# Weights of a network put together from integer halves instead of floating-point products, in a kernel of a gated linear recurrence and a two-layer network

## The chip, the cores and the metric

The kernel runs on one core of a Trainium2 chip. The metric is the time of one launch on the device in microseconds (us), where lower is better. The five engines of a core each work off their own list of instructions, and semaphores hold an instruction until what it needs is there: TensorE (PE) multiplies matrices, VectorE (DVE) and ScalarE (ACT) work element by element, GpSimd (POOL) here clears tiles and issues transfers, and SyncE (SP) only issues transfers.

## The reference

The first half is a recurrence over 768 time steps, for 4 batches and 8 heads of width 48. The second half is a network over the 3072 tokens that come out of it:

```python
f = 1.0 / (1.0 + np.exp(-f_logit))
for t in range(S):
    state = f[:, :, t, :, None] * state + np.einsum('bhd,bhe->bhde', k[:, :, t], v[:, :, t])
    y[:, :, t] = np.einsum('bhd,bhde->bhe', q[:, :, t], state)
...
h = x @ w_in                                          # x is y as (3072, 384); w_in is (384, 2048)
g = np.maximum(h, 0.0) + alpha * np.minimum(h, 0.0)
return (g @ w_out).astype(np.float32)                 # w_out is (2048, 384)
```

`q`, `k`, `v`, `f_logit` and `alpha` are float32. `w_in` and `w_out` are float64, and they arrive in the kernel as 64-bit words which the kernel has to turn into float32 values.

## The kernel before, in words

**Steps.** Time is cut into 6 chunks of 128, and the batches into 2 pairs, which makes 12 steps. Each step has four stages: `prepare` makes products of the decay gates and scaled copies of `q` and `k` (on DVE and ACT); `carry` multiplies across the blocks of a chunk (`off`) and updates the state (`pd`, and `moved`, which writes the state into the tile `vs` on DVE); `attend` computes the scores inside the blocks (`raw`, `qu`), copies them to `A`, multiplies `A` with `vs` (`py`), copies the result to `y` and moves `y` into `xT`, the layout of the network, with ten small transfers (L600 to L608). `network` then computes `ph` = x @ w_in for eight pairs of 128 columns (f0 to f7, L620), the function in the middle with one instruction on ACT (`neg`, L625) and two on DVE (`gate`, L627), and the product with w_out as seven half products that are combined (L655 to L687; the sums of gates that it needs are `sums`, L692). The network of step 0 alone is computed plainly (`po`, L640).

**Order.** PE, DVE and ACT execute in an order that is written out by hand: strings in L726 to L732, one for each of the steps 0 to 3, and one, `usual`, for all others. A letter takes the next piece of a stage: `P` prepare of this step and `Q` of the next, `O` carry, `S` attend, `n` the network of the step before, `a` and `b` the pieces of w_in and w_out on ACT (`uppers`, L232), `w` and `v` the same on DVE (`rests`, L237), `W` the sums of quarters of w_out. A number repeats the letter. The orders of SP and POOL are not written by hand; they follow from where the calls stand in the program.

**Weights.** Each matrix comes in 8 pieces of 128 x 768 words (767 KB, tile `raw`, four buffers), issued by SP. For each piece ACT makes `pos` and `neg` (L202, L204), DVE subtracts them to `lead` (L210, a bf16 value: sign, exponent and first mantissa bits), cuts it to a `power` of two (L216), multiplies the low word by this power (L223, `rest`), and then adds `lead` and `rest`: on DVE for w_in (L228), and by an accumulating transfer issued on POOL for w_out (L230).

**Start.** POOL clears and fills constant tiles, among them the two `vs` (L154 to L157). The first loads of `f`, `q`, `k` and `vs` are issued on SP (L265, L279). PE runs 40 groups of small matmuls on constants (L746)[...].

**Banks.** `psa` has two buffers of two PSUM banks ("pair"), shared by `raw`, `qu`, `off`, `pd` and `py` in turn; so `qu` of a step can start only when the tile before the last has been read completely, for instance `pd` by `moved`. `psn` has four single banks for the network.

Of the kernel before, what the change touches and what calls it, by code (L numbers as in the profile page):

```python
# [8 lines left out]
F32 = mybir.dt.float32  # L9
I16 = mybir.dt.int16  # L10
U16 = mybir.dt.uint16
BF16 = mybir.dt.bfloat16
I32 = mybir.dt.int32
U32 = mybir.dt.uint32
AF = mybir.ActivationFunctionType
ALU = mybir.AluOpType
# [5 lines left out]
U = 2  # L22
CH = 64
NC2 = C // CH
NB = DB // 4
WP = 768
AT_ONCE = 8
IDLE = 40
RAWS, TOPS, POWERS, LEADS = 4, 3, 1, 4


@with_exitstack
def kernel(
# [30 lines left out]
    nc = tc.nc  # L64
    B, NC, _, HP, _ = qT.shape
    DM = v.shape[-1]
# [6 lines left out]
    W = U * HP * C  # L73
# [15 lines left out]
    const = ctx.enter_context(tc.tile_pool(name="const", bufs=1))  # L89
    work = ctx.enter_context(tc.tile_pool(name="work", bufs=2))  # L90
    staging = ExitStack()
    stage = staging.enter_context(tc.tile_pool(name="stage", bufs=1))
# [3 lines left out]
    def pair(name):  # L96
        return psa.tile([128, 2, 512], F32, tag="pair", name=name)

    def bank(name):
        return psn.tile([128, 512], F32, tag="net", name=name)  # L100
# [8 lines left out]
    nc.scalar.dma_start(out=om, in_=alpha)  # L109


    kr = const.tile([128, W // 4, 4], F32, tag="kr", name="kr")
    nc.gpsimd.memset(kr[:, :, 3:4], 1.0)
    NS = G * (NB + 1) + 1
# [20 lines left out]
    for m in range(1, NB):  # L135
        lo = UO[m] + (4 if m == 1 else 0)
        n = NB - m
# [4 lines left out]
    for half in range(2):  # L142
        for m in range(1, NQ):
            n = NQ - m
# [6 lines left out]

    A = const.tile([128, U, H, C], F32, tag="A", name="A")
    nc.gpsimd.memset(A, 0.0)
    vs = []  # L154
    for bp in range(B // U):
        vs.append(const.tile([128, NC2, U, DM + 16], F32, tag=f"vs{bp}", name=f"vs{bp}"))
        nc.gpsimd.memset(vs[bp], 0.0)  # L157
    ident = const.tile([128, 128], F32, tag="ident", name="ident")
    make_identity(nc, ident)
    nc.gpsimd.tensor_scalar(om, om, -1.0, 1.0, ALU.mult, ALU.add)  # L160
# [7 lines left out]
    def load_weights(dst, src, name):  # L168

        rows_ = NK if dst is w_in_sb else 1  # L180
        pieces_ = dst.shape[1] * dst.shape[2] // WP
        if rows_ == 1:
            dst = dst.rearrange("p a n -> p (a n)").unsqueeze(1)
        width = WP // rows_
        words = src.rearrange("p (a n) -> p a n", a=rows_).bitcast(I16)
        at_once = AT_ONCE if rows_ > 1 else 0
        got = {}

        def of(n):
            return dst[:, :, n * width:(n + 1) * width]  # L190

        def by_row(t):
            return t.rearrange("p (a n) -> p a n", a=rows_)

        def upper(n):
            raw = stage.tile([128, WP, 4], I16, tag="raw", name=f"{name}_raw{n}", bufs=RAWS)
            nc.sync.dma_start(out=raw.rearrange("p (a n) four -> p a (n four)", a=rows_)[:, :, 0:4 * width - 1],
                              in_=words[:, :, 4 * n * width + 1:4 * (n + 1) * width])

            top = raw[:, :, 2]  # L200
            pos = stage.tile([128, WP], I16, tag="pos", name=f"{name}_pos{n}", bufs=TOPS)
            nc.scalar.activation(pos, top, AF.Relu, bias=bias[:, 0:1], scale=8.0)  # L202
            neg = stage.tile([128, WP], I16, tag="wneg", name=f"{name}_neg{n}", bufs=TOPS)
            nc.scalar.activation(neg, top.bitcast(U16), AF.Relu, bias=bias[:, 1:2], scale=8.0)  # L204
            got[n] = raw, pos, neg

        def lead(n):
            raw, pos, neg = got[n]
            t = stage.tile([128, WP], BF16, tag="lead", name=f"{name}_lead{n}", bufs=LEADS)
            nc.vector.tensor_tensor(t, pos.bitcast(BF16), neg.bitcast(BF16), ALU.subtract)  # L210
            got[n] = raw, t

        def power(n):
            raw, t = got[n]
            p = stage.tile([128, WP], BF16, tag="power", name=f"{name}_power{n}", bufs=POWERS)
            nc.vector.tensor_scalar(p.bitcast(I16), t.bitcast(I16), -128, None, ALU.bitwise_and)  # L216
            got[n] = raw, t, p

        def rest(n):
            raw, t, p = got.pop(n)  # L220
            got[n] = t
            low = raw.bitcast(U32)[:, :, 0]
            nc.vector.scalar_tensor_tensor(of(n), by_row(low), 2.0 ** -36, by_row(p), ALU.mult, ALU.mult)  # L223

        def both(n):
            t = by_row(got.pop(n))
            if n < at_once:
                nc.vector.tensor_tensor(of(n), of(n), t, ALU.add)  # L228
            else:
                nc.gpsimd.dma_start(out=of(n), in_=t, accum_op=ALU.add)  # L230

        def uppers():  # L232
            for n in range(pieces_):
                upper(n)
                yield

        def rests():  # L237
            for n in range(pieces_ + 1):
                if n < pieces_:
                    lead(n)  # L240
                if n:
                    rest(n - 1)
                if n < pieces_:
                    power(n)
                if n:
                    both(n - 1)
                yield

        return uppers(), rests()

    def rows(par):
# [257 lines left out]
    def attend(bp, c, x):  # L509
# [6 lines left out]
        for u in range(U):  # L516
            raw = pair(f"raw{u}_{i}")
# [9 lines left out]
            for d in range(4):  # L527
                n = 4 - d
# [11 lines left out]
            if c:  # L540
                for m in range(1, NB):
                    lo = UO[m] + (4 if m == 1 else 0)
                    n = DB - 4 * m
# [4 lines left out]
            else:  # L548
                qv = qu.rearrange("p r (h x) -> p (r h) x", h=HP)
                adh = ad[:, u].rearrange("p r h (a t) -> p (r h) a t", a=2)  # L550
                for m in range(1, NQ):
                    n = 4 * (NQ - m)
                    lo = 4 if m == 1 else VO[m]
                    hi = lo + (DB - 4 if m == 1 else 2 * n)
                    to, of, by = ad[:, u].rearrange("p r h t -> p (r h) t")[:, :, 4:DB], qv[:, :, lo:hi], mhalf[:, lo:hi]
                    by = by.bitcast(I32).unsqueeze(1).broadcast_to((128, H, hi - lo))
                    if m > 1:
                        to = adh[:, :, :, 4 * m:16]
                        of, by = (t.rearrange("p h (a t) -> p h a t", a=2) for t in (of, by))
# [11 lines left out]
        for u in range(U):  # L571
            for hp in range(HP):
                for cc in range(NC2):
                    for par in range(2):
                        hd = 2 * hp + par
# [12 lines left out]
        if not (bp or c):  # L588

            for kt in range(NK):  # L590
                b = bank(f"xt{kt}_{i}")
                pairs = [hp for hp in range(HP) if 2 * D * hp < 128 * (kt + 1) and 2 * D * (hp + 1) > 128 * kt]
                for hp in pairs:
                    o = 2 * D - 2 * D * hp + 128 * kt
                    nc.tensor.matmul(b[:, 0:T], lhsT=dense[:, o:o + 128], rhs=y[:, :, hp],
                                     start=(hp == pairs[0]), stop=(hp == pairs[-1]))
                nc.scalar.copy(xT[:, kt], b[:, 0:T])
            yield
            return
        for hd in range(H):  # L600
            d = hd * D
            while d < (hd + 1) * D:
                n = min((hd + 1) * D, (d // 128 + 1) * 128) - d
                p0 = 64 * (hd % 2) + d - hd * D
                (nc.sync if hd % 2 else nc.scalar).dma_start(
                    out=xT[d % 128:d % 128 + n, d // 128].rearrange("p (u t) -> p u t", u=U),
                    in_=y[p0:p0 + n, :, hd // 2])
                d += n  # L608
# [94 lines left out]
    def halves_of_w_out():  # L703
# [12 lines left out]
        for to, x_, y_, op in ((t3, b22, b12, ALU.subtract), (t2, t3, b11, ALU.add), (t4, t2, b21, ALU.subtract),  # L716
                               (b12, b12, b11, ALU.subtract)):
            for h in range(2):
# [5 lines left out]

    steps = [(bp, c) for c in range(NC) for bp in range(B // U)]
    first = (  # L726
        "P2 a P w P a P2 a w a w O a w S2 Q O S Q w S a Q S w S",
        "P n b P a w a n O b w2 v2 S P b n3 v S b2 S2 v2 n Q b n2 Q O b v b n v2 n v S W Q2 S Q W n Q W n W",
        "n2 S n W n3 S n2 Q O S n O Q2 S n S Q S n Q2 n2",
        "S n2 S Q n2 O n O S2 n3 Q2 S n2 S Q n Q n2 Q",  # L730
    )
    usual = "S n2 S n O n O n Q n3 Q n Q S3 n Q S n Q n Q n"  # L732
    pieces = {key: part for keys, parts in (("aw", load_weights(w_in_sb, w_in, "w_in")),
                                            ("bv", load_weights(w_out_sb, w_out, "w_out")))
              for key, part in zip(keys, parts)}

    pieces["W"] = halves_of_w_out()

    def begin(n):
        if n >= len(steps):  # L740
            return [None] * 4
        x = {}
        return [stage(*steps[n], x) for stage in (prepare, carry, attend, network)]

    with tc.manual_schedule(engines={mybir.EngineType.PE, mybir.EngineType.DVE, mybir.EngineType.Activation}):
        for _ in range(IDLE):  # L746
            nc.tensor.matmul(idle[0:32, 0:8], lhsT=ones[:, 0:32], rhs=ones[:, 0:8], start=True, stop=True)
# [65 lines left out]
```

## Time and profile before

| | |
|---|---|
| time, median of 3 runs | 631.77 us (630.31 to 632.38) |
| profiled execution: its own time | 629.98 us |
| profiled execution: span | 628.2 us, granted clock 0.978 |
| busy: PE / PE weight loads / DVE / ACT / POOL | 590.1 / 525.2 / 512.1 / 248.7 / 58.5 us |
| first ph matmuls, `raw` of step 1 starts | 50.5 us, 61.3 us |
| `po` of step 0 | 86.4 to 109.8 us |
| `raw` of steps 3, 5, 6, 7 starts | 160.2, 254.8, 302.1, 349.5 us |
| last matmul ends | 624.9 us |

The profile is of one execution. Its span is counted from the first to the last instruction. "PE off L447 <- DVE q L371: 11.8, 1, 11.8" in the list of waits says that PE stood 11.8 us in total, once, before the instruction of line 447 that works on `off`, and that the wait ended with DVE's instruction of line 371. A releaser called "issue" means that the profile shows nothing that was waited for. In the slices of the span each digit is the busy share of a fortieth of it (15.7 us) in tenths. In a timeline the columns are start, duration, engine, line, operation, tiles, and in brackets the idle time before it. SPq and ACTq are the times in which SP and ACT issue transfers.

### The profile page before, as it was taken

Reading aid. Unit: us, or ns where it says so; the run is one execution under the profiler, and the core shown is the slowest. Engines: PE = TensorE matmul, PEld = TensorE weight load, DVE = VectorE, ACT = ScalarE, POOL = GpSimd, SP = SyncE. Lnnn points to the kernel's source line nnn. Section 1 sums busy time; section 2 is a strip of 40 time slices with the busy share of each in tenths; the row PEclk is TensorE's granted clock in tenths of the full one; section 3 lists DMA queues with packets and bytes.
Section 4 is the critical chain, followed back from the end, with each engine's and each line's share of the span. In section 5 each row is a group of like instructions: output and inputs, shape, how many; then the busy total and the mean of one; then the engine's idle time right before and its main releaser. Section 6 shows DMA issues by size and latency. Waiting matters only on the chain.

```text
span 628.2 us, 19015 instructions
## 1 busy us (share of the span) xinstructions
PE 590.1 (94%) x8188; PEld 525.2 (84%) x8188; DVE 512.1 (82%) x1035; ACT 248.7 (40%) x466; POOL 58.5 (9%) x107
## 2 busy tenths in 40 slices
PE   2458899998999999999999999999999999999997
PEld 2447776788889889889889889889889889889997
DVE  5999799999888889888888888889888889762261
ACT  5766592343451243244244244244244244223110
POOL 9020123001001001001001001001001000000000
PEclk9958799999999999999999999999999999999999
DMA  7944698223313313313313323323323211201000
GB/s 250 314 142 147 178 291 185 29 64 108 70 59 85 84 38 86 69 52 86 71 50 85 67 56 78 55 74 85 54 68 86 47 41 27 53 3 26 26 0 26
DMA packets 70323, 53.57 MB, mean 85 GB/s; under 512 B 47296, under 2 KB 62144, under 8 KB 70240
## 3 DMA queue, kind: packets, MB, share of 16 engines
q1 hardware_dynamic: 57536, 25.37, 16.1%
q0 software_dynamic: 7312, 24.78, 14.1%
q10 hardware_dynamic: 5392, 2.21, 1.8%
q8 instruction: 65, 1.06, 0.8%
q14 instruction: 18, 0.15, 0.1%
HBM read 36.21 MB, written 4.72 MB: 65 GB/s over the span
## 4 chain that ended last, share of the span: by engine, by line
PE 64%; DVE 17%; ACT 10%; issue 4%; DMA 3%; ACTq 1%; DVEq 0%; SPq 0%
PE ph L620 26%; PE pc L659 9%; PE pa L659 6%; PE pe L659 5%; PE pd L659 5%; PE qu L538 3%; ACT A L566 3%; PE raw L523 3%; DVE S L701 3%; DVE gate L627 3%; DVE qd L290 3%; PE py L577 2%; ACT us L317 2%; DMA xT<-y 2%; PE po L640 2%
## 5 line engine op out<-in xcount | busy, mean ns | idle before, releaser
L620 PE MATMUL ph<-xT,w_in_sb 128*128 128x256 f32 x1152 | 262.2, 385 | 0.9 <-DMA xT<-y 0.9
L620 PEld LDWEIGHTS ph<-xT,w_in_sb 128*128 128x128 f32 x1152 | 217.0, 191 | 34.2 <-issue 3.1
L625 ACT ACTIVATE neg<-ph 128x512 f32<-128x512 f32 x96 | 57.1, 596 | 195.5 <-PE ph L620 148.2
L627 DVE SCALAR_TENSOR_TENSOR gate<-neg,om,ph 128x256 f32<-128x256 f32 x192 | 82.1, 476 | 49.1 <-ACT neg L625 48.9
L659 PE MATMUL pc<-t,S 128*128 128x192 f32 x352 | 61.7, 329 | 0.0
L659 PE MATMUL pa<-w_out_sb,gate 128*128 128x192 f32 x352 | 61.1, 327 | 0.0
L659 PEld LDWEIGHTS pa<-w_out_sb,gate 128*128 128x128 f32 x352 | 57.9, 190 | 0.6
L659 PEld LDWEIGHTS pc<-t,S 128*128 128x128 f32 x352 | 57.3, 190 | 0.6
L422 ACT COPY A<-q 48x512 f32<-48x512 f32 x44 | 27.2, 617 | 52.4 <-DVE q L371 52.0
L544 DVE COPY_PREDICATED ad<-mquad,qu 128x224 f32<-128x224 int32 (+6 forms) x140 | 41.9, 299 | 6.2
L529 DVE COPY_PREDICATED ad<-mraw,raw 128x256 f32<-128x256 int32 (+1 forms) x96 | 42.3, 441 | 3.1 <-PE raw L523 0.6
L566 ACT COPY A<-ad 32x256 f32<-32x256 f32 x96 | 38.5, 401 | 1.8 <-DVE ad L560 0.4
L333 DVE TENSOR_TENSOR us<-us,fs 128x768 f32<-128x768 f32 (+5 forms) x60 | 36.7, 611 | 0.0
L677 ACT COPY o<-pa 128x192 f32<-128x192 f32 x11 | 3.5, 319 | 81.2 <-PE pa L659 74.9
L577 PEld LDWEIGHTS py<-A,vs 128*64 128x64 f32 x768 | 25.8, 145 | 9.6 <-ACT A L566 6.8
L577 PE MATMUL py<-A,vs 128*64 128x64 f32 x768 | 29.2, 233 | 4.9 <-ACT A L566 4.2
L659 PE MATMUL pe<-w_out_sb,S 128*128 128x192 f32 x176 | 30.5, 327 | 2.4 <-ACT o L677 2.4
L659 PEld LDWEIGHTS pe<-w_out_sb,S 128*128 128x128 f32 x176 | 28.8, 190 | 2.7 <-ACT o L677 2.7
L538 PE MATMUL qu<-us,k 48*32 48x112 f32 (+1 forms) x1536 | 27.4, 260 | 3.7 <-issue 3.5
L701 DVE TENSOR_TENSOR S<-gate 128x512 f32<-128x512 f32 x44 | 30.3, 688 | 0.8
L659 PE MATMUL pd<-w_out_sb,S 128*128 128x192 f32 x176 | 30.4, 326 | 0.0
L659 PE MATMUL pb<-t,gate 128*128 128x192 f32 x176 | 30.4, 326 | 0.0
(110 smaller groups left out, 729.7 us busy)
## 6 DMA issues: line engine op xcount, KB each, us to landing
w_out_raw<-in_w_out SPq DMA_DIRECT2D x8, 767.8 KB, 6.6
w_in_raw<-in_w_in SPq DMA_DIRECT2D x8, 767.2 KB, 5.6
f<-in_fT POOLq DMA_DIRECT2D x11, 512.0 KB, 4.8
q<-in_qT POOLq DMA_DIRECT2D x11, 512.0 KB, 4.1
k<-in_kT POOLq DMA_DIRECT2D x11, 512.0 KB, 4.6
out<-o SPq DMA_DIRECT2D x24, 192.0 KB, 2.7
vs<-in_v POOLq DMA_DIRECT2D x22, 192.0 KB, 4.9
w_out_sb<-w_out_lead POOLq DMA_DIRECT2D x8, 384.0 KB, 6.9
```

Of the source, the lines that this page charges most:

```text
L333: nc.vector.tensor_tensor(us[:, :, UO[m]:UO[m] + 4 * n].rearrange("p g (i r) -> p g i r", r=4), us[:, :, skip:skip + 4 * n].rearrange("p g ...
L422: nc.scalar.copy(A[halves(cc)[1], :, par * HP:(par + 1) * HP, CH * cc:CH * (cc + 1)], q3[rows(par)].rearrange("p (u h c) s t -> p u h c (s ...
L529: nc.vector.copy_predicated(adu[:, :, :, d:4], mraw[:, d, :, d:4].bitcast(I32).unsqueeze(1).broadcast_to((128, H, NB, n)), rv[:, :, QO[d]: ...
L538: nc.tensor.matmul(qu[DB * j:DB * (j + 1), par, hp * QS + 4:hp * QS + QL], lhsT=k4[r_, g * DB:(g + 1) * DB], rhs=us[r_, g, 4:QL], start=Tr ...
L544: nc.vector.copy_predicated(ad[:, u, :, :, 4 * m:DB], mquad[:, lo:lo + n].bitcast(I32).unsqueeze(1).unsqueeze(1).broadcast_to((128, 2, HP, ...
L566: nc.scalar.copy(A[s_, u, :, s_], ad[s_, u].rearrange("p r h t -> p (r h) t"))
L577: nc.tensor.matmul(py[64 * par:64 * par + 64, u, o:o + CH], lhsT=vs[bp][:, cc, u, hd * D:hd * D + 64], rhs=A[:, u, par * HP + hp, CH * cc: ...
L620: nc.tensor.matmul(ph[:, j * T:(j + 1) * T], lhsT=w_in_sb[:, kt, m * 128:(m + 1) * 128], rhs=xT[:, kt], start=(kt == 0 and j == 0), stop=( ...
L625: nc.scalar.activation(neg, phv, AF.Relu, scale=-1.0)
L627: nc.vector.scalar_tensor_tensor(gate[:, m % NH, m // NH], neg[:, j], om[:, m:m + 1], phv[:, j], ALU.mult, ALU.add)
L659: nc.tensor.matmul(to[:, 0:DH], lhsT=of(f), rhs=by(f), start=(f == 0 and not more), stop=(f == NH - 1), skip_group_check=True)
L701: nc.vector.tensor_tensor(to, x_, y_, op)
```

## The change

It has six parts. (1) ACT gets a third instruction for each piece: it scales the low word by 2^-13 and rounds it to a 32-bit integer in the final weight tile. `power` and `rest` on DVE are gone, and `both` adds `lead`, read as a 16-bit integer, to the upper half of each 32-bit weight. (2) This holds for w_out too, so its eight accumulating transfers on POOL are gone. (3) The two `vs` tiles are cleared on DVE at the very beginning instead of on POOL. (4) 56 instead of 40 groups of small matmuls run at the start. (5) The ten transfers to `xT` go round SP, ACT, POOL, SP, ACT instead of SP and ACT in turn. (6) All five order strings are new.

```diff
-AT_ONCE = 8
-IDLE = 40
-RAWS, TOPS, POWERS, LEADS = 4, 3, 1, 4
+IDLE = 56
+RAWS, TOPS, LEADS = 4, 3, 4
...
+    vs = []
+    for bp in range(B // U):
+        vs.append(const.tile([128, NC2, U, DM + 16], F32, tag=f"vs{bp}", name=f"vs{bp}"))
+        nc.vector.memset(vs[bp], 0.0)
+
     kr = const.tile([128, W // 4, 4], F32, tag="kr", name="kr")
...
-    vs = []
-    for bp in range(B // U):
-        vs.append(const.tile([128, NC2, U, DM + 16], F32, tag=f"vs{bp}", name=f"vs{bp}"))
-        nc.gpsimd.memset(vs[bp], 0.0)
...
+            nc.scalar.activation(as_int(n, I32), by_row(raw.bitcast(U32)[:, :, 0]), AF.Copy, scale=2.0 ** -13)
             got[n] = raw, pos, neg
 
+        def as_int(n, dtype):
+            t = of(n).bitcast(dtype)
+            return t if dtype is I32 else t.rearrange("p a (n two) -> p a n two", two=2)[:, :, :, 1]
...
-        def power(n):
-            raw, t = got[n]
-            p = stage.tile([128, WP], BF16, tag="power", name=f"{name}_power{n}", bufs=POWERS)
-            nc.vector.tensor_scalar(p.bitcast(I16), t.bitcast(I16), -128, None, ALU.bitwise_and)
-            got[n] = raw, t, p
-
-        def rest(n):
-            raw, t, p = got.pop(n)
             got[n] = t
-            low = raw.bitcast(U32)[:, :, 0]
-            nc.vector.scalar_tensor_tensor(of(n), by_row(low), 2.0 ** -36, by_row(p), ALU.mult, ALU.mult)
 
         def both(n):
-            t = by_row(got.pop(n))
-            if n < at_once:
-                nc.vector.tensor_tensor(of(n), of(n), t, ALU.add)
-            else:
-                nc.gpsimd.dma_start(out=of(n), in_=t, accum_op=ALU.add)
+            t = by_row(got.pop(n).bitcast(I16))
+            nc.vector.tensor_tensor(as_int(n, I16), as_int(n, I16), t, ALU.add)
...
+        queues = iter([nc.sync, nc.scalar, nc.gpsimd, nc.sync, nc.scalar] * 2)
...
-                (nc.sync if hd % 2 else nc.scalar).dma_start(
+                next(queues).dma_start(
...
     first = (
-        "P2 a P w P a P2 a w a w O a w S2 Q O S Q w S a Q S w S",
-        "P n b P a w a n O b w2 v2 S P b n3 v S b2 S2 v2 n Q b n2 Q O b v b n v2 n v S W Q2 S Q W n Q W n W",
-        "n2 S n W n3 S n2 Q O S n O Q2 S n S Q S n Q2 n2",
-        "S n2 S Q n2 O n O S2 n3 Q2 S n2 S Q n Q n2 Q",
+        "P5 a w P a2 O w S w a w a2 S Q S O S w Q2 S Q2 S w",
+        "a2 w b w O w n2 b2 v S P v2 n2 S b v Q n b n O S2 v n b v n Q2 b v Q b n S v2 W Q W S n2 W n W",
+        "n S P n2 S n W n O Q n3 O S Q n S Q n S Q2 S Q n3",
+        "S n3 P S Q S n O n O n4 Q S Q S Q n S Q n3",
     )
-    usual = "S n2 S n O n O n Q n3 Q n Q S3 n Q S n Q n Q n"
+    usual = "S n2 O P n S Q n2 Q n3 O n S2 n Q S Q2 S n3"
```

## The prediction

> **What bounds the kernel now.** I read the share of busy time first, then the slices of the span.
>
> ```profile
> PE 590.1 (94%) x8188; PEld 525.2 (84%) x8188; DVE 512.1 (82%) x1035; ACT 248.7 (40%) x466; POOL 58.5 (9%) x107
> ...
> PE   2458899998999999999999999999999999999997
> ...
> DVE  5999799999888889888888888889888889762261
> PEclk9958799999999999999999999999999999999999
> ```
>
> TensorE (PE) is the bound: 628.2 - 590.1 = 38 us idle, and the windows place 31 us of it before 130 us, 2.4 at 155 to 157.5, about 1.2 from 160 to 580, and 3.2 behind the last matmul. A usual step repeats every 47.33 us (`raw` starts at 254.78 and 302.11) with some 47.24 of it matmuls. So there are two places to look at: the first 130 us, where something can be won, and the usual step, where at most 0.1 us can be won but anything late costs seven times (steps 4 to 10). VectorE (DVE) reads 9 in nearly every early slice, so it looks like the bound there. The waits say what PE stood for, and where ACT did:
>
> ```profile
> PE off L447 <- DVE q L371: 11.8, 1, 11.8
> ...
> PE off L457 <- issue: 5.5, 2, 3.8
> ...
> PE qu L538 <- issue: 3.5, 2, 2.0
> ...
> ACT w_in_pos L202 <- DMA w_in_raw<-in_w_in: 3.2, 1, 3.2
> ...
> PE pe L659 <- ACT o L677: 2.4, 1, 2.4
> ```
>
> The first is step 0's own preparation on DVE, which the change leaves. The fourth has its origin on SP's queue, the fifth on ACT's (timelines of the two):
>
> ```profile
> 2.26 0.69 SPq L197 DMA_DIRECT2D w_in_raw<-in_w_in  x1
> 8.61 1.31 SPq L279 DMA_DIRECT2D vs<-in_v  x2
> 9.96 12.91 SPq L197 DMA_DIRECT2D w_in_raw<-in_w_in  x4
> ```
>
> ```profile
> 150.90 5.90 ACTq L605 DMA_DIRECT2D xT<-y  x5
> 157.14 0.32 ACT L677 COPY o<-pa 128x192 f32<-128x192 f32 x1 [6.27 <-DMA xT<-y]
> ```
>
> The `vs` loads wait on SP until POOL has cleared `vs` (8.61); the second weight piece stands behind them and lands at 16.05. At 150.9 ACT needs 5.9 us to issue five transfers and only then copies `pa`, for which `pe` waits. Five issues take 0.6 us each; single issues in step 4 show a gap from 245.00 to 248.25 before the fifth, just after the first landings at 248.0: the 9th and 10th of the ten transfers wait until the first ones land.
>
> **What the Trainium skill says.** "VectorE: DVE Perf Modes", What auto-detection actually checks: a two-source operation runs two elements a cycle only when every tensor is 16-bit with step 1 or -1. The trace agrees: `lead` (bf16, contiguous) takes 551 ns, the f32 add of 768 elements 952. The new int16 add has step 2, so it should be a 952. "DMA: Bandwidth & Descriptors", Issuing engines are not separate DMA queues: a third queue saves issue time on the sequencer and no transfer time; the trace shows landings after 4.9 us (median) against 0.6 us for an issue. "TensorE: Matmul & The Clock Gate", Part 1: an idle window halves the clock. PEclk shows it: 0.51 at 40 to 50 us and 0.50 at 60 to 70.
>
> **The parts.**
> *Weights, DVE.* Each of 16 pieces loses `power` (0.36) and `rest` (0.95). `both` stays at 0.95 for w_in's eight and is new on DVE for w_out's eight. Starts follow each other about 0.09 closer than durations. w_in: 8 x 1.31 = 10.5 us less; w_out: 8 x (0.36 + 0.95 - 0.95) = 2.9 less. DVE gains 13 us. Unknown is the int16 add: 0.5 if it ran packed, 1.9 at double; I take 0.95.
>
> *Weights, ACT.* A third instruction per piece, a Copy of 768 without a bias pointer. Copies of 512 take 0.590 and of 1024 1.042 (rows `ksn` and `qd`), so between them 0.82; "ScalarE: Activation LUTs", What ACT_TABLE_LOAD costs, prices 186 + 0.833 x 768 = 826 ns, an estimate. Bounds 0.72 and 1.05 (pos measures 0.99). 16 x 0.82 = 13 us more on ACT: the work is not removed, it changes engine. It stands in front of `A`, `us` and `y` copies there, so in the first 60 us it is not free.
>
> *Accumulating transfers.* Eight of 384 KB leave POOL's queue (6.9 us to landing). They compete with the xT transfer of 110 us, which took 7.75 us to land and cost PE 0.9.
>
> *Memsets of vs.* From POOL (1.43 us each) to DVE's head. "VectorE: DVE Perf Modes", Zero memsets, says one cycle an element: 1600 elements, about 1.7 us each, an estimate no row here shows. DVE first works at 4.2 us, waiting for `lvl` and `f`: 3.4 fits. Without that cover it would cost its 3.4. SP then goes f, q, k, vs, raws without a stop: raw 1 can land near 10 instead of 16, and ACT's 3.2 us wait falls away.
>
> *IDLE 56.* 16 more groups at the start, while PE waits for `off` until 21 anyway. The 3.84 us "issue" stall at 21 to 24.8 falls on the first long run of matmuls while DMA is 0.9 busy[...]. I let it vanish, but `off` itself is not the end of that chain, so it counts zero. Bounds 0 and -2.
>
> *Step 0 walked through.* ACT is now the chain from `A<-q` at 20.6: pieces 1, 2 (2 x 2.55) to 25.9; off and ksn copies to 28.8; pieces 3 to 5 (7.5) to 36.3; f, kr, qd to 39; `A<-ad`, vs, `A<-ad` to 43.2; `us` to 45.3; y to 46.4; xT to 51.6; pieces 6, 7 and w_out's first (7.6) to 59.2; `off` evicted 61.1, and `raw` of step 1 at 61.2 against 61.34. Nothing is won up to here: ACT took back what DVE gave. What is won comes after it, while PE runs the 36 `ph` matmuls and `po` of step 0: the 2.04 us `qu` L538 <- issue stall at 63 (the same shift of fetches as above), the half clock at 60 to 70 us in which 36 `ph` matmuls took 10.24 us instead of 8.0, and the 0.9 for xT; together 5.2, of which I count 4.5 because the half clock follows idle time that may move and not go. `po` ends at about 105.5 instead of 109.8. Gain 4.5, bounds 2 (half clock and xT wait stay or move) and 6 (a `raw` 1 us earlier).
>
> *n = 2.* L677 now follows four issues (2.8 us; no slot to wait for), so the 2.4 us stall goes. DVE, with w_out's adds and W behind it, may hold qu1 up by 1.0. Gain 1.4, bounds 0 and 2.4.
>
> *xT on three queues.* SP 4, ACT 4, POOL 2. ACT's issue falls from 5.9 to 2.8 us, which in a usual step hides nothing (L677 at 297.02, `pe` at 299.42). POOL's two stand behind the `vs` loads, which wait for `py`; landing at about 47 + 2 against need at 49.0 within the period. Zero, bounds 0 and 0.5 a step.
>
> *The usual order.* This is the row I distrust. Lines of DVE in the step at 254.78:
>
> ```profile
> 280.87 2.48 DVE L627 SCALAR_TENSOR_TENSOR gate<-neg,om,ph 128x256 f32<-128x256 f32 x6
> ...
> 291.89 0.36 DVE L672 TENSOR_TENSOR Csum<-pc,Csum 128x192 f32<-128x192 f32 x1 [1.45 <-PE pc L659]
> ...
> 296.85 1.12 DVE L501 TENSOR_TENSOR vs<-vs,pd 48x384 f32<-48x384 f32 x2
> ...
> 303.91 0.43 DVE L529 COPY_PREDICATED ad<-mraw,raw 128x256 f32<-128x256 int32 x1
> ```
>
> Gates of f7 end 28.6 us into the step, and pa's last weights (its matmuls start 26.5 in, 2.6 long) need them at 28.5 to 28.7: no slack already. In the new order the `A<-q` copies (2.5 us, ACT) stand before neg f2 and Q1 (3.64) before gates f3; I find f7's gates at 29.0, 0.3 to 0.5 late. `moved(1)` now comes after Q3, Q4 and Q5: from L672 at 34.45, 3.13 + 3.66 + 4.45 + 2.1 + the 0.27 of L676 = 13.6, to 48.0; `qu` u0 of the next step takes the pair that `moved(1)` frees and would start at 47.92. So 0.1 to 0.2 late. DVE has 4.7 us of slack in a step (42.4 of 47.3 us), so lateness isn't carried on. Together 0.4 a step, x 7 = 2.8 us lost; bounds 0 and 8. The drained steps 11 and 12 and the tail stay.
>
> **Sum.** -4.5 - 1.4 + 2.8 = -3.1 us. The profiled execution took 629.98 (span 628.2 and 1.8 around it), so 626.9; the median of the runs lies 1.8 above the profiled one, 631.77 - 3.1 = 628.7. I say 628.5.
>
> **Rivals.**
> *Slower side: DVE's late moved(1) and gates bound every usual step.* Place: `qu` u0 of steps 5 to 11 and pa's last weights. It decides when DVE's chain ends over 1.0 us late a step: 7 x 1.1 = 7.7 lost against 4.5 won in the prologue if the n = 2 gain is eaten by qu1: 631.77 + 3.2, about 635. For it: both slacks are already nil or below. Against it: DVE has 4.7 us idle a step, which the new order may place better than I see.
>
> *DVE bounds the first 70 us.* Then 13 us less work on it is worth 8 to 10, giving about 622. For it: the 9s. Against: ACT's walk above, which is full from 20.9 on.
>
> *ACT takes back everything, or the int16 add runs at 1.9.* Each 0.1 us more on the Copy costs 0.9 on the nine pieces before step 1; at 1.05 it costs 2, the usual loss 2.8, so the time stays within a microsecond of 631.8.
>
> **Chances.** Forecast (623.5 to 629.8): 0.46. More, as in the second rival: 0.12. Unchanged: 0.18. Slower: 0.24. A measurement of this kernel tells about 0.3% (1.9 us) from nothing. Faster 0.58, same 0.18, slower 0.24. The range goes from 621.5 (most of the larger gain) to 636 (most of the slower rival), and leaves 0.2; the likeliest case alone has 623.5 to 629.8.
>
> **What would show it.** Right: no ACT wait for w_in_raw; ACT without gaps from 21 to 60; `raw` of step 1 within 1 us of 61.3; po's end 4 to 5 us earlier; no pe wait at 155; steps of 47.7 in place of 47.33, with PE waiting for DVE before pa or qu. Wrong: steps of 47.3 or below (then 625.5 or so), or above 48.2 (then slower); int16 adds far from 0.95 or Copies far from 0.82; a `raw` of step 1 that moves by several us either way.

## The result, and the profile after

The changed kernel takes 627.39 us (median of 5 runs, 626.62 to 628.11) against 630.58 us for the kernel before (median of 5 runs that now include the three shown above, 629.81 to 632.38). The ratio is 0.9943, with a 95% interval of 0.9923 to 0.9962: 0.57% faster. Its profiled execution took 627.25 us with a span of 625.4 us, 2.8 us shorter than the one of before.

The page of the changed kernel, shares of busy time and slices of the span:

```profile
PE 590.1 (94%) x8220; PEld 525.8 (84%) x8220; DVE 502.5 (80%) x1013; ACT 265.3 (42%) x482; POOL 60.5 (10%) x119
...
PE   3458999999999999999999999999999999999997
...
DVE  7599889999799599699699699699799789663261
ACT  5797893361442542442443343353253253222110
PEclk9996999999999999999999999999999999999999
```

DVE lost 9.6 us of busy time and ACT gained 16.6; PE's busy time is what it was. DVE reads 5 in the second slice (16 to 31 us), where it read 9, and ACT reads 9 in the third (31 to 47 us), where the page of before has a 6. The list of waits, the lines in which PE or the weights figure:

```profile
PE off L432 <- DVE q L356: 9.3, 1, 9.3
...
PE raw L508 <- ACT A L450: 5.2, 1, 5.2
...
PE pd L472 <- issue: 2.4, 1, 2.4
...
PE qu L523 <- DVE vs L486: 2.0, 5, 0.4
...
PE qu L523 <- DVE ad L529: 1.3, 1, 1.3
```

There is no wait of ACT for `w_in_raw` any more, and none of `pe` for L663 (the old L677). Three new ones stand there: PE for ACT in step 0 (5.2 us), PE for DVE in step 2 (1.3 us, at 118.2), and `qu` for `moved(1)` in five usual steps, 0.4 us each. (The diff of the change further up has a slip in the string of step 2: the kernel that ran ends it with `Q n S Q n Q S2 Q n3`.)

The two places that the prediction showed, in the timelines of SP and ACT of the changed kernel:

```profile
2.56 1.42 SPq L264 DMA_DIRECT2D vs<-in_v  x2
4.02 20.28 SPq L196 DMA_DIRECT2D w_in_raw<-in_w_in  x6
```

```profile
149.58 2.82 ACTq L591 DMA_DIRECT2D xT<-y  x4
152.50 0.32 ACT L663 COPY o<-pa 128x192 f32<-128x192 f32 x1 [2.95 <-DMA xT<-y]
```

And the end of a usual step on DVE, with the `qu` that stands behind it on PE:

```profile
285.82 0.36 DVE L658 TENSOR_TENSOR Csum<-pc,Csum 128x192 f32<-128x192 f32 x1 [0.72 <-PE pc L645]
...
298.40 1.12 DVE L486 TENSOR_TENSOR vs<-vs,pd 48x384 f32<-48x384 f32 x2
...
300.75 0.35 DVE L672 TENSOR_TENSOR o<-pe,o 128x192 f32<-128x192 f32 x1
```

```profile
298.25 0.92 PE L508 MATMUL raw<-qd,k 48*32 48x80 f32 x64
299.58 1.11 PE L523 MATMUL qu<-us,k 48*32 48x112 f32 x64 [0.41 <-DVE vs L486]
```

How the start of `raw` moved from the kernel before to the changed one shows where the time went (us, the two profiles):

| | before | after | difference |
|---|---|---|---|
| `raw` of step 1 | 61.34 | 64.80 | +3.5 (`ph` of f0 and f1 are done by then in both) |
| start of the first `po` | 86.39 | 84.57 | -1.8 |
| `ph` behind the last `po` | 109.61, and 0.89 of wait for xT in it | 107.42, no wait | -2.2, with the wait -3.1 |
| `raw` of step 3 | 160.31 | 156.36 | -3.95 |
| `raw` of step 5 | 254.78 | 250.65 | -4.13 |
| `raw` of step 10 | 491.55 | 489.02 | -2.53 |
| start of the last product `pe` | 622.08 | 619.35 | -2.73 |

Between steps 5 and 10 a step takes 47.67 us instead of 47.35. From the start of `raw` of step 1 to the first `po`, with the same matmuls in both kernels, PE takes 19.8 us instead of 25.1. What makes `raw` of step 1 late is seen on PE (timeline of the changed kernel):

```profile
55.95 1.97 PE L459 MATMUL pk<-ident,ks 128*128 128x128 f32 x8
57.71 7.17 PE L606 MATMUL ph<-xT,w_in_sb 128*128 128x256 f32 x24
64.80 0.92 PE L508 MATMUL raw<-qd,k 48*32 48x80 f32 x64
```

The granted clock is 0.67 in these 10 us (50 to 60). At full clock 24 such matmuls take 5.45 us, for instance from 66.24 on.

### The profile page after: what moved, and what is told of

It is laid out like the page before. It is cut to its first block, busy times and chain, and to the rows that moved or that the text cites. A ratio compares the mean times of both kernels' runs of the same rounds, so it can differ in the third digit from the quotient of the medians.

```text
span 625.4 us, 19119 instructions
## 1 busy us (share of the span) xinstructions
PE 590.1 (94%) x8220; PEld 525.8 (84%) x8220; DVE 502.5 (80%) x1013; ACT 265.3 (42%) x482; POOL 60.5 (10%) x119
## 4 chain that ended last, share of the span: by engine, by line
PE 70%; DVE 19%; ACT 8%; issue 1%; DMA 1%; ACTq 0%; DVEq 0%
PE ph L606 37%; PE pa L645 8%; PE pc L645 7%; PE pb L645 4%; PE qu L523 3%; PE pe L645 2%; PE pd L645 2%; DVE us L318 2%; PE raw L508 2%; PE py L562 1%; PE pd L472 1%; DVE q L356 1%; DVE us L309 1%; DVE k L335 1%; DVE vs L486 1%
## 5 line engine op out<-in xcount | busy, mean ns | idle before, releaser
L645 PE MATMUL pa<-w_out_sb,gate 128*128 128x192 f32 x352 | 63.4, 333 | 0.0
L645 PE MATMUL pc<-t,S 128*128 128x192 f32 x352 | 60.9, 326 | 0.0
L514 DVE COPY_PREDICATED ad<-mraw,raw 128x256 f32<-128x256 int32 (+1 forms) x96 | 42.4, 442 | 8.3 <-PE raw L508 5.8
L551 ACT COPY A<-ad 32x256 f32<-32x256 f32 x96 | 38.6, 402 | 1.4
L571 ACT COPY y<-py 128x512 f32<-128x512 f32 x24 | 12.9, 592 | 58.1 <-PE py L562 58.1
L302 ACT COPY us<-qd 128x256 f32<-128x256 f32 x48 | 29.8, 675 | 7.6 <-DVE qd L275 7.5
L508 PEld LDWEIGHTS raw<-qd,k 48*32 48x32 f32 x1536 | 18.3, 109 | 14.3 <-issue 8.7
L508 PE MATMUL raw<-qd,k 48*32 48x80 f32 x1536 | 23.3, 243 | 7.1 <-ACT A L450 5.2
```

What stands on the lines that cost most here:

```text
L302: nc.scalar.copy(q4[:, :, :, r], qdv[r][:, :, :, 0])
L508: nc.tensor.matmul(raw[DB * j:DB * (j + 1), par, hp * C:hp * C + QW], lhsT=k[r_, g * DB:(g + 1) * DB], rhs=qd[r_, g], start=True, stop=True)
L514: nc.vector.copy_predicated(adu[:, :, :, d:4], mraw[:, d, :, d:4].bitcast(I32).unsqueeze(1).broadcast_to((128, H, NB, n)), rv[:, :, QO[d]: ...
L551: nc.scalar.copy(A[s_, u, :, s_], ad[s_, u].rearrange("p r h t -> p (r h) t"))
L645: nc.tensor.matmul(to[:, 0:DH], lhsT=of(f), rhs=by(f), start=(f == 0 and not more), stop=(f == NH - 1), skip_group_check=True)
```

## The experiments

Each was timed in five rounds beside the kernel before, whose median in these rounds was 630.8 to 631.0; the number beside each result is its ratio to the kernel before with the 95% interval. The changed kernel stands at 0.9943.

**The usual order undone.** Only the last two lines of the order change.

```diff
-        "S n3 P S Q S n O n O n4 Q S Q S Q n S Q n3",
+        "S n3 P S Q S n O n O n4 Q S Q S Q n S Q n3 Q",
...
-    usual = "S n2 O P n S Q n2 Q n3 O n S2 n Q S Q2 S n3"
+    usual = "S n2 S n O n O n Q n3 Q n Q S3 n Q S n Q n Q n"
```

> The changed kernel with the usual order of the kernel before (and one more Q at the end of step 3's string, which that order needs). Theory (the new usual order loses about 0.4 us a step because qu waits for moved(1)): the waits of qu for L486 are gone, steps fall from 47.67 to 47.35 us, and the time from 627.4 to about 625.2 us. Rival (the new weights and queues also need the new usual order, for instance because xT is late): a new wait in every usual step, and 627.4 or more.

Measured: 625.41 us, 0.9924 (0.9906 to 0.9942). `raw` starts at 296.91, 344.33 and 391.70, steps of 47.4, and no `qu` waits for L486. The theory held: the new usual order costs 1 to 2 us (2.0 between the medians, 1.2 between the two ratios to the kernel before), and the new weights and queues do not need it.

**moved(1) put earlier.**

```diff
-    usual = "S n2 O P n S Q n2 Q n3 O n S2 n Q S Q2 S n3"
+    usual = "S n2 O P n S Q n2 Q n3 O n S2 n Q S2 Q2 n3"
```

> The changed kernel with one piece moved in the usual order: the last piece of attend (y, moved(1), the xT transfers) before the last two pieces of the coming step's prepare instead of after them, so that on VectorE moved(1) runs some 5 to 8 us earlier. Theory (the 0.41 us wait of qu in five or six steps is moved(1) alone): steps of 47.3, the time about 2 us below the changed kernel, 625.3. Rival (VectorE is simply late as a whole and another instruction is waited for next, such as the q3 product that the score copies need): below 0.7 us gained.

Measured: 630.22 us, 1.0005 (0.9992 to 1.0018), 2.8 us slower than the changed kernel, so the theory fell in this form. The wait of `qu` is gone, but the next one is longer (waits of PE, and the timelines of DVE and PE, of this run):

```profile
PE ph L606 <- DVE Csum L667: 6.9, 6, 1.2
```

```profile
291.16 0.95 DVE L482 TENSOR_TENSOR vs<-vs,f 48x768 f32<-48x768 f32 x1 [0.95 <-PE py L562]
...
301.72 0.35 DVE L667 TENSOR_TENSOR Csum<-pc,Csum 128x192 f32<-128x192 f32 x1
```

```profile
302.13 5.45 PE L606 MATMUL ph<-xT,w_in_sb 128*128 128x256 f32 x24 [1.22 <-DVE Csum L667]
```

`moved(1)` now stands at DVE's head before `py` is through, so DVE idles 0.95 us, and everything behind it is that much later. The last in line are the combinations of the half products, and L667 frees the bank that `ph` of f0 takes. In the changed kernel that instruction ended at 300.2, 0.4 us ahead of `ph`. The rival was right: the step's end has two releases to serve, a pair for `qu` and a bank for `ph`, and moving one alone makes the other late.

**Both releases ahead of the fifth piece.** The end of the usual order is mixed so that `moved(1)` and the combinations both come before the 4.4 us of the fifth piece of `prepare`.

```diff
-    usual = "S n2 O P n S Q n2 Q n3 O n S2 n Q S Q2 S n3"
+    usual = "S n2 O P n S Q n2 Q n3 O n S2 n Q S Q S n2 Q n"
```

> The changed kernel with the end of the usual order mixed on VectorE: the fourth piece of prepare, then y and moved(1), then the combinations of the half products, then the fifth piece, then the last combination. The run that put moved(1) first made the combinations 1.2 us late for the bank of ph f0; here both come before the fifth piece (4.4 us). Theory (the loss of a usual step is which of VectorE's releases come last, not its amount of work): no wait of PE for L486 or L667, steps of 47.3, about 625.2 us as with the old usual order. Rival (VectorE's list is too long for the end of the step in any order that begins with Q pieces this late): some wait of 0.3 us or more a step remains, 627 or more.

Measured: 624.91 us, 0.9909 (0.9894 to 0.9924). Steps of 47.3 (`raw` at 296.95, 344.33, 391.53, 438.88), no wait of PE for L486 or L667 in a usual step. So it is which release comes last that costs, and not the amount of work on DVE, which is the same in this and the two kernels above.

**xT on two queues again.**

```diff
-        queues = iter([nc.sync, nc.scalar, nc.gpsimd, nc.sync, nc.scalar] * 2)
+        queues = iter([nc.scalar, nc.sync] * 5)
```

> The changed kernel with the xT transfers on SyncE and ScalarE in turn, as before. The prediction priced three queues at zero in a usual step. Theory A (that price holds, and only step 2 gains): 2.4 us lost once, 629.8. Theory B (the new order has py later, so that y is copied 5 us before pe instead of 10, and ScalarE's five issues of 5.9 us delay L663, for which pe waits): about 2 us lost in each of eight steps, 16 us, 643 us, with PE waiting at pe for L663.

Measured: 629.85 us, 0.9988 (0.9972 to 1.0004). The size is that of theory A and the mechanism that of theory B:

```profile
PE pe L645 <- ACT o L663: 5.5, 7, 1.5
```

`pe` waits in seven steps, 0.3 to 1.5 us each, and not in step 2 alone (there 0.51). ACT's five issues took 4.2 to 5.3 us in these seven steps, where step 2 of the kernel before had 5.9. The transfers land sooner in the new order (2.7 us in the median against 4.7), which fits the prediction's reading that the last issues wait for the first landings. The waits of `qu` for L486, 2.0 us in the changed kernel, are gone in this run, so the two do not add: on balance the third queue is worth 2.5 us in the new order, a little in each step.

**Three queues alone in the kernel before.**

```diff
+        queues = iter([nc.sync, nc.scalar, nc.gpsimd, nc.sync, nc.scalar] * 2)
...
-                (nc.sync if hd % 2 else nc.scalar).dma_start(
+                next(queues).dma_start(
```

> The kernel before with the xT transfers on three queues alone. Theory (ScalarE's issue falls from 5.9 to 2.8 us, and only step 2 has pe waiting behind it): 2.4 us faster than before, 628.2 to 628.6, no wait of pe for L677 left. Rival (the wait passes on to the next instruction, for instance to VectorE's combinations or to xT behind GpSimd's vs loads): below 1 us gained.

Measured: 631.4 us, 1.0007 (0.9994 to 1.002). The rival held. ACT's issues did fall to 2.8 us and `pe` no longer waits, but in the same step PE then stands for DVE (timeline of PE of this run):

```profile
162.75 1.08 PE L538 MATMUL qu<-us,k 48*32 48x112 f32 x64 [0.94 <-DVE us L333]
165.08 5.45 PE L621 MATMUL ph<-xT,w_in_sb 128*128 128x256 f32 x24 [1.26 <-DVE Csum L682]
```

0.94 + 1.26 = 2.2 of the 2.4 us are back: DVE must have been about 2 us late in the kernel before too, where the stall covered it. From the start of `pe` of step 2 to the next `pe` this run takes 49.42 us, where the kernel before takes 46.95.

**Fewer groups at the start.** `IDLE = 40` in place of 56.

> The changed kernel with 40 instead of 56 groups of small matmuls at the start. Theory (these only move the places where PE's stalls named issue fall): the three stalls named issue of the changed kernel (0.6 at 32.9, 2.4 at 36.9, 1.3 at 55.2) move to other instructions, and the time changes by less than 1 us, 626.4 to 628.4. Rival (the extra groups took away the 3.8 us stall that the kernel before had at 21 us): the stall is back, raw of step 0 starts later, and the time rises by 2 us or more.

Measured: 626.8 us, 0.9947 (0.9926 to 0.9969), no difference. The rival's stall did come back: PE's waits of this run show `off` L442 <- issue with 4.8 us, 3.7 of them at once, and the 5.2 us wait of `raw` for ACT that the changed kernel has is only 1.25 us here: the stall lies in the same time. `raw` of step 0 starts at 27.85 us, as in the changed kernel (27.77), so PE stood for ACT's list either way.

**The integer weights alone, in the kernel before.** Its function `load_weights` is replaced by the new one (parts 1 and 2 of the change, the diff above), all else stays.

> The kernel before with the integer weights alone (parts 1 and 2 of the change; order strings, memsets, 40 groups and two queues as before). Theory (ScalarE takes back in the first 60 us what VectorE gives, and the order around it is the old one): raw of step 1 within 1.5 us of 61.3, the time within 2 us of the kernel before. Rival (VectorE was the bound of the first 70 us): 4 to 8 us faster.

Measured: 634.86 us, 1.0063 (1.0046 to 1.0081): 0.6% slower than the kernel before. Neither theory allowed for this. `raw` of step 1 starts at 67.28 instead of 61.34: ACT's additional Copies stand before `off`'s evictions, and PE waits for these (`raw` <- ACT A L449, 3.64 us at step 0 and 1.86 at step 1), while DVE, relieved of 10.9 us of busy time, stands for `lead`'s inputs (6.4 us). ACT also waits 6.0 us for `w_in_raw`, in two waits, but that is no effect of the new weights: the profile of the three-queue run above, which has the old ones, shows the same 6.0 us and `raw` of step 1 at 64.60. Beside that profile the integer weights are 2.7 us later, about as much as the three Copies (0.9 us each) that ACT makes from 59 us on, ahead of the evictions of `off` of step 1. So about 3 of the 4 us are placed, in ACT's Copies, and the remaining 1 us stays open. (That both profiles are 3.3 us or more behind that of the kernel before at this place is not the weights' doing: the three-queue run shows it without them.)

**The floating-point weights in the changed kernel.** Its `load_weights` is replaced by the old one.

> The changed kernel with the weights put together as before (power, rest, and w_out's accumulating transfers on GpSimd). Theory (the weights are worth little by themselves, the gain is order and queues): 1 to 3 us slower than the changed kernel, 628.5 to 630.5. Rival (the new order needs the 13 us that VectorE was given): VectorE is full past 70 us, moved and the gates are late in the first three steps, 633 or more.

Measured: 637.86 us, 1.011 (1.0094 to 1.0126), 10.5 us slower than the changed kernel, and the rival held, though in part elsewhere than it said. Half of the loss is there at `raw` of step 1, which starts at 69.57 us and not at 64.80 (timelines of ACT and SP and waits of PE in this run):

```profile
38.50 0.98 ACT L203 ACTIVATE w_in_pos<-w_in_raw,bias 128x768 int16<-128x768 int16 x1 [7.37 <-DVE ad L561]
```

```profile
24.38 10.74 SPq L198 DMA_DIRECT2D w_in_raw<-in_w_in  x3
```

```profile
PE pd L488 <- issue: 5.3, 1, 5.3
...
PE py L578 <- ACT A L567: 4.8, 2, 4.5
...
PE po L642 <- DMA w_out_sb<-w_out_lead: 1.7, 1, 1.7
```

The instruction named as the releaser of ACT's 7.37 us is not the cause: it belongs to another chain and ends at 38.6. The sixth piece needs the `raw` buffer of the second, which in this form is read last by DVE's `rest`; that ended at 31.9, SP issued the load at 31.98 (the second of the three issues shown), and it landed 6.4 us later, at 38.39. With the new weights ACT is the last reader and frees the buffer itself. So the order, in which ACT takes six pieces before `y`, stands on that, and `f`, `A` and `y` were queued behind the 7.4 us. (At 66.14 ACT has stood another 7.0 us, for a `pos` buffer that DVE's `lead` frees.) (DVE's own time for a piece, 2.6 us against 1.4, did not fill it: it was idle 2.7 us at 38.6.) From `raw` of step 1 to `raw` of step 2 another 4.5 us are lost: the granted clock is 0.83 from 60 to 80 us, so that 24 `ph` matmuls take 6.90 us and not 5.45, and `po` waits 1.7 us for one of w_out's accumulating transfers. `raw` of step 3 starts at 166.03 instead of 156.36. So neither the weights nor the rest of the change is a gain by itself: +4.0 and +7.0 us, and together -3.2. What the new form is worth for w_in and for w_out singly was not run.

**Two pieces put into ACT's gap.** The trace of the changed kernel shows ACT idle from 13.8 to 19.84 us, waiting for DVE's `q` product, with the words of pieces 1 and 2 landed at 14.3 and 16.8:

```profile
19.84 1.25 ACT L407 COPY A<-q 48x512 f32<-48x512 f32 x2 [6.06 <-DVE q L356]
```

```diff
-        "P5 a w P a2 O w S w a w a2 S Q S O S w Q2 S Q2 S w",
+        "P5 a3 w P O w S w a w a2 S Q S O S w Q2 S Q2 S w",
```

> The changed kernel with w_in's pieces 1 and 2 moved on ScalarE ahead of the score copies of step 0 (A from q), into the 6.1 us in which ScalarE waits for these; the pieces' words have landed at 14.3 and 16.8 us. Nothing else moves. Theory (ScalarE's list is the chain from 20 us to raw of step 1): everything on ScalarE after 21 us is about 5 us earlier, so y at about 41 instead of 45.6 and raw of step 1 at about 60 instead of 64.8; the time 3 to 5 us lower, 622.5 to 624.5. Rival (VectorE's list is as long, since the preparation of step 1 stands on it): below 1.5 us gained.

Measured: 624.23 us, 0.9896 (0.988 to 0.9913), 3.2 us less than the changed kernel. `raw` of step 1 starts at 60.00, as expected, but in part for another reason. `y` is only 2.2 us earlier (43.44 for 45.60), since PE stands 3.1 us at `raw` of step 0 for nothing that the profile names, DVE's copies of that `raw` come before the next `lead` in its list, and the sixth piece on ACT needs one of three `pos` buffers that this `lead` frees: it ends at 31.5, ACT goes on at 31.62 after 2.3 us. So `pk` starts 2.15 us earlier. The other 2.7 of the 4.8 us are clock: it is full in this execution (granted 1.00 from 40 to 60 us, where the profile of the changed kernel has 0.89 and 0.67), and `pk` and `ph` of f0 and f1 take 1.09 and 5.35 us for 1.97 and 7.17. The run with both order edits below repeats the edit at a clock like that of the old-usual-order run (`ph` 5.86 and 5.81 us), and there `raw` of step 1 is 2.6 us earlier, 61.06 for 63.62. So ACT's list is what step 0 waits for, and of the 5 us taken out of it 2.2 to 2.6 reached `pk`, and about 3 the end.

**vs cleared on GpSimd again.** The two memsets stand at their old place on POOL.

> The changed kernel with the two vs tiles cleared on GpSimd at their old place, so that SyncE's queue stands again until GpSimd is through. The prediction counted ScalarE's 3.2 us wait for the second weight piece as gone with this part. Theory from the trace of the changed kernel (ScalarE waits there 6.1 us for VectorE's q product in any case, to 19.8 us, so an earlier landing is not used): raw of step 1 within 0.5 us of 64.8, time within 1 us of 627.4. Rival (the later weight pieces then land too late for ScalarE's full list after 21 us): 1.5 us or more slower, with ScalarE waiting for w_in_raw.

Measured: 626.98 us, 0.9943 (0.9925 to 0.996), no difference. SP issues the second piece at 10.14 and it lands at 15.82, but ACT waits for DVE's `q` to 19.90 anyway and stands for no piece afterwards. By itself this part of the change is worth nothing in the new order.

**Both gains, and one more.** The two order edits that gained were joined. A second run also moved one group of `ph` in step 2, to fill the 1.3 us wait of `qu` there; the diff shows this second run's further line.

```diff
-        "n S P n2 S n W n O Q n3 O S Q n S Q n Q S2 Q n3",
+        "n S P n3 S W n O Q n3 O S Q n S Q n Q S2 Q n3",
```

> The changed kernel with both order edits that gained alone: pieces 1 and 2 of w_in ahead of the score copies of step 0, and the mixed end of the usual order. Theory (the two places are independent, one before 65 us and one in every usual step): the gains add, 3.2 + 2.5 us below 627.4, so 621 to 622.5. Rival (a start 4 us earlier makes another engine late in steps 1 to 3 and part is given back): above 623.

Measured: 621.97 us, 0.9866 (0.9846 to 0.9887). The gains add (3.2 + 2.5 expected, 5.4 measured), and this kernel beats both, by 1.3% the one before and by 0.9% the changed one.

> As the run with both order edits, and in step 2 one more group of ph matmuls (f3, 2.7 us) before the second raw and qu, which waited 1.3 us for VectorE's copies of the first, late because of the sums of quarters of w_out (3.56 us at 110.7). Theory (that wait is only a matter of where VectorE's burst falls): the 1.3 us wait goes and the time is about 1 us below the run with both edits. Rival (VectorE is full from 70 to 155 us, so the wait comes back at a later instruction of step 2): no difference.

Measured: 622.89 us, 0.9879 (0.9858 to 0.9901), no gain. The wait of `qu` is gone, and `off` waits instead, 1.90 us for DVE's copies in `ad` (L514, at 122.2). The rival held: DVE is full in these steps, and the wait only moved.

## Why the prediction was right, and where its steps were off

The forecast was 628.5 us, 3.3 less than the 631.77 of then; the measured gain is 3.2. The time lies in the range, and in the likeliest case's own. But the sum has two terms that were each too large, with opposite signs, and it came out right partly by that luck. Of the signs that it named, these came: no ACT wait for `w_in_raw`, no `pe` wait at 155, steps of 47.67, and PE waiting for DVE before `qu`. These failed: `raw` of step 1 moved by 3.5 us, which it had named as a sign of being wrong, and `po` ended 2.2 us earlier and not 4 to 5. ACT is not wholly without gaps either: from 46.7 to 51.4 us it waits three times 1.3 us for PE's `xt`.

*ACT takes over as the chain of step 0.* Right. The walk had `y` at 46.4 and `off` of step 1 evicted at 61.1; the trace has the end of `y` at 46.7 and the end of `off`'s copies at 60.9, with ACT without a gap from 19.84 to 46.7. The early pieces confirmed it: shortening ACT's list alone gained 3.2 us. What the walk left out is what PE and DVE do in that time. From 45.5 to 56 us it is DVE's preparation of step 1, which cannot begin before ACT's `us` copies, and then `pk` and `ph` on PE, that stand on the chain.

*The prologue's gain, -4.5 and -1.4 at n = 2.* Direction right, size too large: `raw` of step 3 is 3.95 us earlier and not 5.9. The step that failed is "together 5.2, of which I count 4.5", with nothing lost up to `raw` of step 1. Behind `raw` of step 1 the gains came as described: the stall of 2.04 us at `qu` and the slow `ph` of 10.24 us are gone, and PE needs 5.3 us less up to `po`. But the lowered clock came back ahead of `raw` of step 1, and there `pk` and `ph` of f0 and f1 lost 2.6 us to it. How much of the clock returns differs between single executions. The two-queue run has the same program up to there and comes to `pk` at 56.00, and its clock is full (timeline of PE):

```profile
56.93 5.35 PE L606 MATMUL ph<-xT,w_in_sb 128*128 128x256 f32 x24
62.20 0.92 PE L508 MATMUL raw<-qd,k 48*32 48x80 f32 x64
```

There `raw` of step 1 is within 1 us of 61.3, `po` ends at about 105, and `raw` of step 3 starts at 154.98, 5.3 us earlier than in the kernel before. So the term is near what an execution at full clock gives. In the changed kernel, whose five runs show mean clocks of 0.991 to 0.997, it is not reached; what decides it was not tested. (The stall named issue of 1.34 us in `off` of step 1 is nothing new: the kernel before had one of 1.66 us there.) The n = 2 term was about right: the wait of 2.4 us went and 1.31 of it came back as the `qu` wait that the text priced at 1.0.

*The usual order, +2.8.* The mechanism is exactly that of the forecast, with half the size. `qu` waits for `moved(1)` in five steps at 0.41 us, where 0.1 to 0.2 was the price, and DVE's chain after L658 ran to 299.5, 48.9 us after `raw`, where 48.0 was worked out. The gates' lateness of 0.3 to 0.5 us showed with 0.2 at most: `pa` behind `pd` runs 2.87 to 3.06 us in these steps, where its undisturbed length is 2.87. Together 1.2 us were lost between step 3 and the end. Undoing the order gained 2.0, mixing its end 2.5. (DVE's slack of 4.7 us does not follow from 42.4 of 47.3, which leaves 4.9; the windows of the kernel before have DVE 41.3 us busy in such a step. Nothing else rests on it.)

*Prices.* The Copy took 0.89 (w_in) and 0.92 us (w_out) in the mean and not 0.82, the int16 add 1.05 and not 0.95, a memset of `vs` 1.39 and not 1.7. DVE's busy time fell by 9.6 us and not 13: the 16 adds at 0.1 more make 1.6, and the memsets that came over 2.8, which the prediction had priced but left out of its 13. ACT's rose by 16.6, of which 14.4 are Copies (eight of 0.893 and eight of 0.917).

*What was costed at nothing.* The memsets and IDLE at nothing: right, both were undone without effect. The SP queue's early pieces: also nothing, but the sentence that ACT's wait falls away with it misses that ACT waits for DVE's `q` in the same time; only in the run with the early pieces is the landing used. The third queue at zero in a usual step: wrong. In the new order `y` comes nearer to `pe`, and two queues cost 2.5 us over seven steps. Read from the order of before, where L677 had 2.4 us to spare, this could not be seen; it had to be read from the new one.

*The rivals.* "DVE bounds the first 70 us", with 8 to 10 us to win, is refuted for the order of before: the integer weights alone, which take 10.9 us from DVE, made that kernel slower by 4 us. What happened there is "ACT takes back everything", and ACT took back more than that. The order, in turn, needs weights whose buffers ACT frees: the prediction treated the parts as if they added, and they do not (+4.0, +7.0, together -3.2). The slower side's mechanism, late releases on DVE, was real and cost about 0.3 us a step, below the 1.0 from which it would have decided.

## What to carry to other kernels

When work moves from one engine to another, time the parts together: an order of instructions fits one division of the work, and a part that is a loss alone can be the condition of a gain. Before you price a stall as gone, look which engine was late behind it; in three of these runs (`moved(1)` earlier, three queues alone, one more group of `ph`) a removed wait came back behind another instruction, nearly as long or longer. Before you read a gain from one profile beside another, look at the granted clock in the same stretch of both: here it made up more than half of a gain of 4.8 us. And at the end of a loop's step, list every release that the next step needs, with its time on the releasing engine: putting both of two releases ahead of a long block won what moving one of them lost.

## What the runs showed of the hardware that was not expected

An int16 addition whose destination and first operand take every second half word (step 2, 768 elements; the second operand is contiguous) took 1047 ns, 10% more than the float32 addition of as many elements (952 ns). The Copy from 32-bit unsigned to 32-bit signed integers took 0.89 and 0.92 us in the mean, where copies of float32 interpolate to 0.82.

With 40 small groups of matmuls at the start a stall of PE named "issue" falls behind the 79th matmul of `off`'s second product of step 0 in all four profiles (3.84 us in the kernel before, 3.74 in the run with fewer groups, 3.86 with the integer weights alone, 5.10 with three queues alone); with 56 groups none of the profiles has one there. So the number of matmuls ahead moves these stalls; what they are was not tested.

The same 24 matmuls `ph` of f0 and f1 took 5.35 to 7.42 us in seven profiles (the changed kernel and the six runs that leave its order up to there alone), in all of which PE came to `pk` between 55.95 and 56.12 us. The granted clock from 50 to 60 us lay between 0.67 and 1.00 in them. So it differs between executions of the same instructions.
